# Denser side work in the first feed-forward, and split score products for four more head pairs

## The chip, the cores and the metric

The kernel runs on one core of one Trainium2 chip. The metric is the device time of one execution in microseconds; the time before is the median of three runs. The engines are TensorE (PE; its weight loads are listed as PEld), VectorE (DVE), ScalarE (ACT), GpSimd (POOL) and SyncE (SP), which issues the transfers.

## The reference, cut to what matters

```python
# attention over 8 batches, 12 heads, 448 tokens, head size 64, all float32
q_n, k_n = rmsnorm(q, g_q), rmsnorm(k, g_k)
scores = (q_n @ k_n.T) / sqrt(64)
attn = softmax(scores)
x = (attn @ v), heads side by side: (8, 448, 768)
# spectral mix, then a feed-forward layer
u = x + real(fft2(x))                  # over tokens and channels
un = (u - mean(u)) / sqrt(var(u) + 1e-6)
out = u + relu(un @ w_ch1) @ w_ch2     # 768 -> 3072 -> 768
```

## The kernel before, in words

**Batches and pairs.** Each of the eight batches goes through `aux` (attention, then the spectral mix) and then `ffn`. Attention works on six pairs of heads per batch. For a pair, `transpose_pair` loads q, k and v, normalizes q and k, turns them with TensorE and leaves `QT` and `KD`; `softmax_pair` makes the scores of four chunks of 112 tokens, with a minimum on DVE and an exponential on ACT for each head; `value_pair` turns the probabilities and multiplies them with v. `fold` and `spectral` do the Fourier part: products y, ab, transposes x, then the normalized rows `un`, whose sum of squares ACT takes in place over `u` after `u` has been stored to memory.

**Split and plain products.** A float32 value is cut into a rounded part and a remainder (type fp32r), and a product is made as a sum of fast products. In a split pair of scores (lines 322 to 348) ACT makes two rounded copies of q, two scaled ones of k and two copies of these into the other half, DVE makes two remainders of q and two of k; the remainder of k lies in one buffer that all pairs share, `KL`. The scores are two matmuls per head and chunk (line 375). In a plain pair (lines 302 to 320) ACT makes one copy of each, and the scores are one float32 matmul per head and chunk (line 372), which the trace shows as two instructions. Before the change, pairs 2 to 5 of the first batch are plain, by `PLAIN_SCORES`, which `plain_s` reads. The products with v are plain in batches 0 and 1 whatever that constant says (`PLAIN_PAIRS`).

**Feed-forward.** `ffn(b)` has 24 `up` products (line 908, 18 matmuls each) and 36 `down` products (line 929, 12 each), in six groups: one up first, then four ups and six downs per group, the last group with three ups. In `ffn(0)` the weights arrive as 64-bit floats and are converted piece by piece (`convert`, lines 701 to 730): a load into one of two buffers, two passes on ACT, three on DVE, one on POOL, one on ACT, one on DVE, and a store of the result (`kept`, line 758) for the later batches. 60 pieces are needed; 14 are converted during the first batch's attention.

**The order of the work.** `ffn(b)` is the main work, and `aux(b + 1)` is merged into it as side work. Both are generators that yield planned costs; an up counts 3420, a down 2280. The rule is in `merge`:

```python
done += cost
while side_done < done * ratio:
    x = next(side, None)
...
for _ in side:
    pass
```

What is left of the side work when the feed-forward is through runs behind it. The ratio is `RATIO_FIRST` for `ffn(0)` and `RATIO` (0.49) for the others. Before the merge, `AHEAD` = 14 steps of the second batch's side work are done along with the first batch's spectral mix. After `ffn(b)`, `ffn_input(b + 1)` turns the `un` rows for the next feed-forward. The framework orders the instructions of each engine by this program order and a planned timeline, when the kernel is built; on the chip each engine and SP's queue takes its instructions in that order.

Of the kernel before, what the change touches and what calls it, by code (L numbers as in the profile page):

```python
# [24 lines left out]
NPAIR = H // 2  # L25
# [12 lines left out]


RATIO = 0.49  # L40
RATIO_FIRST = 0.45
CONVERT_EARLY = 0.12
EARLY = 2
DFT_STEP = 40
AHEAD = 14
PLAIN_PAIRS = range(2 * NPAIR)
PLAIN_SCORES = range(2, NPAIR)
PACE = 3
LAG = 3

# [39 lines left out]
def spectral_block(ctx, tc, q, k, v, g_q, g_k, w1, w2, d1, d2, out, nb=B):  # L90
# [197 lines left out]
    def plain_s(b, p):  # L288
        return b * NPAIR + p in PLAIN_SCORES

# [396 lines left out]
    def aux(b):  # L687

        EO, uns[b] = [], {}
        yield from attention(b, EO)  # L690
        mixing.append(b)
        yield from spectral(b, xTs[b], EO, uns[b])
# [296 lines left out]
    for b in range(nb):  # L989
        merge(  # L990
            ffn(b, ffn_input(b, uns.pop(b))),
            second if b == 0 else aux(b + 1) if b + 1 < nb else iter(()),
            RATIO if b else RATIO_FIRST,
        )
# [21 lines left out]
```

## Time and profile before

| | |
|---|---|
| median of three runs | 2202.68 us (2202.3 to 2204.17) |
| the profiled execution's own time | 2202.25 us |
| its span, first to last instruction | 2200.5 us |
| mean granted TensorE clock | 0.977 |
| busy: PE, DVE, ACT, POOL | 96%, 70%, 48%, 16% |

The profile names groups of instructions by line, engine, operation and tile. A busy PE is not PE at its peak, since matmuls are pipelined and their ends are modelled: how fast TensorE really goes is read from the starts of its instructions. The stretch up to about 190 us is the first batch's attention and spectral mix; from there to 472.6 us is `ffn(0)`; from about 506 us each batch takes some 250 us.

### The profile page before, as it was taken

The page shows a single profiled execution, that of the slowest core. Times are in us where ns is not written, and L with a number is a line of the kernel's source. Part 1 is how long each engine was busy: PE and PEld are TensorE (multiplying, and loading weights), DVE is VectorE, ACT ScalarE, POOL GpSimd, SP SyncE. Part 2 cuts the span into 40 slices and gives each one's busy share as a digit, 9 for nine tenths or more (in the row PEclk, how much of TensorE's full clock was granted, in tenths as well). Part 3 has the DMA queues.
Part 4 walks back from the last instruction along what each step waited for, and adds up shares of the span by engine and source line. Part 5 has one row for each costly group of instructions (what it writes and reads, how often), then busy time and mean ns, then how long its engine had stood idle before and what let it go on. Part 6 is the DMA issues. An engine that isn't in the chain of part 4 may idle for free.

```text
span 2200.5 us, 31296 instructions
## 1 busy us (share of the span) xinstructions
PE 2118.1 (96%) x11224; PEld 1841.3 (84%) x11224; DVE 1541.8 (70%) x2987; ACT 1046.3 (48%) x2242; POOL 344.2 (16%) x196
## 2 busy tenths in 40 slices
PE   7977999989999999999999999999999999999997
PEld 4345777767999999999999999999999999998997
DVE  6678778766887588857787588857787588753122
ACT  7757766635553455525553355525553355422100
POOL 3323433311110011101110011101110011000000
PEclk8987999999999999999999999999999999999999
DMA  5546887846555675558556675568556674449665
GB/s 164 170 134 205 271 277 242 259 149 185 169 170 188 190 216 174 167 184 245 170 166 187 187 227 164 167 189 246 171 160 189 199 215 155 155 167 283 214 212 138
DMA packets 298301, 424.74 MB, mean 193 GB/s; under 512 B 186609, under 2 KB 224482, under 8 KB 298146
## 3 DMA queue, kind: packets, MB, share of 16 engines
q1 hardware_dynamic: 298146, 422.74, 62.9%
q8 instruction: 89, 1.46, 0.3%
q14 instruction: 66, 0.54, 0.1%
HBM read 362.89 MB, written 65.27 MB: 195 GB/s over the span
## 4 chain that ended last, share of the span: by engine, by line
PE 82%; DMA 5%; ACT 4%; DVE 4%; issue 1%; POOL 1%; SPq 1%; DVEq 0%; ACTq 0%; POOLq 0%
PE h L908 29%; PE o L929 29%; PE S L375 5%; PE av L483 4%; PE pt L471 4%; DMA dblw<-w 3%; PE av L449 2%; PE y L588 2%; PE qk L327 1%; ACT P L113 1%; PE pt L442 1%; DMA ur<-u_dram 1%; PE oT L874 1%; PE x L620 1%; DMA w<-w 1%
## 5 line engine op out<-in xcount | busy, mean ns | idle before, releaser
L929 PE MATMUL o<-hs,w 128*128 128x448 f32 x3456 | 790.3, 371 | 4.7 <-DMA w<-w 1.9
L908 PE MATMUL h<-unT,w 128*128 128x448 f32 x3456 | 776.8, 371 | 5.1 <-ACT unT L113 2.8
L908 PEld LDWEIGHTS h<-unT,w 128*128 128x128 f32 x3456 | 642.4, 189 | 58.9 <-ACT unT L113 3.7
L929 PEld LDWEIGHTS o<-hs,w 128*128 128x128 f32 x3456 | 638.4, 189 | 63.0 <-issue 3.8
L113 ACT ACTIVATE P<-S,mn 112x448 f32<-112x448 f32 x384 | 243.6, 637 | 199.5 <-DVE mn L113 182.4
L113 ACT ACTIVATE hs<-h 128x448 fp32r<-128x448 f32 x192 | 104.4, 544 | 323.5 <-PE h L908 322.1
L113 DVE TENSOR_REDUCE mn<-S 112x1 f32<-112x448 f32 x384 | 234.0, 619 | 30.9 <-PE S L375 27.0
L113 DVE SCALAR_TENSOR_TENSOR hs<-h,hs 128x448 fp32r<-128x448 f32 x192 | 119.4, 622 | 147.6 <-ACT hs L113 145.6
L113 DVE TENSOR_TENSOR acc<-o,acc 128x448 f32<-128x448 f32 x240 | 149.0, 621 | 103.1 <-PE o L929 100.5
L113 POOL TENSOR_TENSOR qkn<-raw 112x1024 f32<-112x1024 f32 x36 | 68.5, 1902 | 700.3 <-PE qk L327 431.8
L113 POOL TENSOR_TENSOR ss<-ss,nhalf 112x16 f32<-112x16 f32 x48 | 147.0, 3062 | 184.5 <-DVE ss L113 165.9
L113 ACT CAST T<-pt 128x448 fp32r<-128x448 f32 x216 | 112.9, 533 | 100.7 <-PE pt L471 99.2
L483 PE MATMUL av<-T,vhl 128*128 128x448 f32 x432 | 153.6, 384 | 0.1
L113 DVE TENSOR_TENSOR T<-pt,T 128x448 fp32r<-128x448 f32 x216 | 131.8, 619 | 27.4 <-ACT T L113 26.3
L375 PE MATMUL S<-KD,QT 128*112 128x448 f32 x352 | 138.7, 395 | 7.0 <-ACT bs L113 4.0
L375 PE MATMUL S<-rounded,QT 128*112 128x448 f32 x352 | 132.0, 376 | 0.0
L113 DVE TENSOR_SCALAR P<-P,sm 112x448 f32<-112x448 f32 x288 | 122.1, 462 | 4.2
L471 PE MATMUL pt<-ident,P 112*128 112x112 f32 x864 | 121.4, 259 | 0.0
L471 PEld LDWEIGHTS pt<-ident,P 112*128 112x128 f32 x864 | 102.4, 140 | 15.5
L726 POOL TENSOR_TENSOR magw<-magw,dblw 128x512 uint32<-128x512 uint32 (+1 forms) x46 | 78.9, 1716 | 156.0 <-DVE magw L722 97.9
L113 POOL TENSOR_TENSOR rstd<-st,nhalf 112x1 f32<-112x1 f32 (+2 forms) x32 | 19.5, 608 | 522.5 <-DVE st L113 508.1
L483 PEld LDWEIGHTS av<-T,vhl 128*128 128x128 f32 x432 | 80.8, 188 | 7.6 <-DVE T L113 0.5
(122 smaller groups left out, 2495.4 us busy)
## 6 DMA issues: line engine op xcount, KB each, us to landing
w<-w SPq DMA_DIRECT2D x192, 768.0 KB, 4.7
w<-w SPq DMA_DIRECT2D x288, 512.0 KB, 4.2
dblw<-w SPq DMA_DIRECT2D x28, 512.0 KB, 5.0
dblw<-w SPq DMA_DIRECT2D x18, 768.0 KB, 5.6
raw<-q SPq DMA_DIRECT2D x96, 112.0 KB, 3.6
raw<-k SPq DMA_DIRECT2D x96, 112.0 KB, 3.7
v<-v SPq DMA_DIRECT2D x96, 96.0 KB, 4.2
u_dram<-u SPq DMA_DIRECT2D x24, 336.0 KB, 2.9
```

The source lines that it names most:

```text
L113: ins = emit(*args, **kwargs)
L327: nc.tensor.transpose(pt[:, c * C : (c + 1) * C], qk[:, i, c].rearrange("t h d -> t (h d)"), ident[:C, :C],)
L375: ins = nc.tensor.matmul(s_, QT[:, h, cs], K[:, h], start=step == 0, stop=step == 1)
L442: nc.tensor.transpose(pt[:, c * C : (c + 1) * C], Pc[c][:, 512 * h + j * 128 : 512 * h + (j + 1) * 128], ident[:C, :C],)
L449: nc.tensor.matmul(av[:D, :S], vhl[:, j, h], T, start=j == 0, stop=False)
L471: nc.tensor.transpose(pt[:, c * C : (c + 1) * C], Pc[c][:, 512 * h + j * 128 : 512 * h + (j + 1) * 128], ident[:C, :C],)
L483: nc.tensor.matmul(av[:, :S], lv, T[:, i], start=(j == 0 and i == 0), stop=False)
L588: nc.tensor.matmul(o, src[:, par, t0 : t0 + n], D1[:, ri, par, cols], start=i != 1, stop=i != 0,)
L620: nc.tensor.transpose(xp[:n, i * 128 : (i + 1) * 128], src[:, 3 * half + i], ident)
L726: behind(nc.gpsimd.tensor_tensor(out=bits, in0=bits, in1=low, op=ALU.add))
L908: pace(nc.tensor.matmul(o, w[:, a, c], unT[c][:, z], start=n == 0, stop=n == 17))
L929: pace(nc.tensor.matmul(o, w[:, a, f], hs[4 * g + f][:, z], start=n == 0, stop=n == 11))
```

## The change

Two constants change. `RATIO_FIRST` goes from 0.45 to 0.6, and `PLAIN_SCORES` is empty, so that pairs 2 to 5 of the first batch take the split way of lines 322 to 348 and 374 to 379.

```diff
 RATIO = 0.49
-RATIO_FIRST = 0.45
+RATIO_FIRST = 0.6
 CONVERT_EARLY = 0.12
...
 PLAIN_PAIRS = range(2 * NPAIR)
-PLAIN_SCORES = range(2, NPAIR)
+PLAIN_SCORES = ()
 PACE = 3
```

## Rows read from the trace of the kernel before

**Rows 1.** The page, busy time of TensorE: share of the span, instructions.

```profile
PE 2118.1 (96%) x11224; PEld 1841.3 (84%) x11224; DVE 1541.8 (70%) x2987; ACT 1046.3 (48%) x2242; POOL 344.2 (16%) x196
```

**Rows 2.** Windows: stretch, length, busy PE, PEld, DVE, ACT, POOL, clock, DMA, GB/s.

```profile
189.50:472.60 283.10, 273.54 (x1284) 210.57 (x1284) 219.81 (x358) 182.16 (x349) 106.92 (x61) 0.98 0.79 258
...
189.50:390.00 200.50, 190.95 (x903) 147.81 (x904) 160.90 (x258) 139.86 (x268) 80.04 (x46) 0.97 0.80 266
...
472.60:505.90 33.30, 19.92 (x113) 16.28 (x114) 20.92 (x51) 15.33 (x32) 2.33 (x4) 0.87 0.27 79
...
750.00:1000.00 250.00, 249.88 (x1398) 229.27 (x1397) 189.76 (x382) 118.97 (x263) 31.95 (x17) 1.00 0.63 190
```

**Rows 3.** Timeline of TensorE, last down of the first feed-forward, early up of the second.

```profile
469.90 2.70 PE L929 MATMUL o<-hs,w 128*128 128x448 f32 x12
...
505.94 1.47 PE L908 MATMUL h<-unT,w 128*128 128x448 f32 x3
```

**Rows 4.** Timeline of TensorE in the second feed-forward: y first and last, un.

```profile
714.81 1.93 PE L588 MATMUL y<-D,eo 128*113 128x130 f32 x16
...
719.76 0.32 PE L588 MATMUL y<-D,tot 128*112 128x65 f32 x2
...
751.79 1.04 PE L820 MATMUL un<-ident,un 113*128 113x113 f32 x9
```

**Rows 5.** Chain of waits, 390 to 420 us: start, length, what.

```profile
401.31 0.77 PE pt L442 x8
402.08 3.67 PE h L908 x18
405.75 0.81 PE S L375 x4
...
410.21 1.65 PE av L449 x4
...
416.61 2.47 PE o L929 x12
```

**Rows 6.** SP's queue, 184 to 480 us: conversion loads, and its longest wait.

```profile
L709 SPq DMA_DIRECT2D dblw<-w x44: 367/384/921, 184.4 to 438.1; - x44
...
SPq L758 <- DVE w L728: 91.3, 34, 7.0
```

**Rows 7.** Groups of the whole kernel by shape, making of QT, KD and KL.

```profile
L113 DVE SCALAR_TENSOR_TENSOR rounded<-qk,gains,KD 64x448 fp32r<-64x448 f32 x88 | 60.0, 681 | 19.1 <-ACT KD L113 17.7
L113 ACT ACTIVATE KD<-qk,gains 64x448 fp32r<-64x448 f32 x88 | 55.5, 631 | 44.7 <-PE qk L327 32.6 <-DVE rounded L113 9.3
L113 DVE TENSOR_TENSOR QT<-qk,QT 64x448 fp32r<-64x448 f32 x88 | 54.8, 622 | 9.3 <-ACT QT L113 7.2
L113 ACT CAST KD<-KD 64x448 fp32r<-64x448 f32 x88 | 49.8, 565 | 2.4
L113 ACT CAST QT<-qk 64x448 fp32r<-64x448 f32 x88 | 46.4, 527 | 18.8 <-PE qk L327 18.3
L113 ACT ACTIVATE KD<-qk,gains 128x448 f32<-128x448 f32 x4 | 2.6, 642 | 0.0
L113 ACT COPY QT<-qk 128x448 f32<-128x448 f32 x4 | 2.2, 561 | 0.2 <-PE qk L307 0.2
```

**Rows 8.** First batch's attention: window of its plain pairs, timeline of plain scores.

```profile
43.20:146.90 103.70, 90.59 (x356) 37.87 (x354) 74.39 (x126) 77.85 (x172) 33.34 (x21) 0.92 0.50 150
...
89.77 1.76 PE L372 MATMUL S<-KD,QT 64*112 64x448 f32 x8
```

**Rows 9.** Timelines of DVE and POOL, 52 to 84 us; chain of waits at 488 us.

```profile
52.86 0.68 DVE L722 SCALAR_TENSOR_TENSOR magw2e<-dblw2e,magw2e 128x512 uint32<-128x512 uint32 x1
...
81.91 2.25 DVE L722 SCALAR_TENSOR_TENSOR magw2e<-dblw2e,magw2e 128x512 uint32<-128x512 uint32 x1
...
81.77 1.83 POOL L726 TENSOR_TENSOR magw1e<-magw1e,dblw1e 128x768 uint32<-128x768 uint32 x1 [5.83 <-DVE magw1e L722]
...
488.66 2.74 DMA u_dram<-u
```

## The prediction

> **What bounds the kernel now.** I read the busy times first: TensorE is busy for 96% of the span [rows 1], which says that it is the bound, but a busy PE can also be a slow one. So the windows come next. In the steady part PE is busy for 249.88 of 250 us at full clock [rows 2]: there every microsecond of TensorE work is one of time, and the change touches none of it. It touches two places in front of that, and each must be read by its own limit.
>
> The first is the stretch of ffn(0), 283.1 us, and the 33.3 us behind it [rows 2]. What TensorE needs there at full speed comes from the spacing of its instructions [rows 5]: 18 up matmuls take 3.67 us, 12 down matmuls 2.47, four instructions of a plain product with v 1.65 (0.90 per matmul where they stand in pairs; I take 0.45 an instruction), four score matmuls 0.81, eight transposes 0.77. By the code ffn(0) has 24 x 18 ups and 36 x 12 downs, 177 us. Six pairs of plain products with v are 96 instructions (two per matmul), 43 us; five pairs of scores, 80 matmuls, 16 us; some 240 transposes, 23 us. That is 259 of 283 us, so **24 us of TensorE time are lost inside ffn(0)**, though it shows as busy.
>
> Behind it, from the last down product to the first real up of the next feed-forward, 33.3 us pass [rows 2, 3]. What TensorE does there is the second batch's spectral mix: y, 5.3 us when nothing holds it up [rows 4], ab and x, 12 and 24 instructions, 4.7 us by rows 5; then un, 2.3 us, and 8 score matmuls of the third batch, 1.6 us. That is 14 us, so **19 us are lost in the gap**. At later boundaries un stands among the down products [rows 4], and nothing is lost.
>
> The code says why the gap is there. The second batch's side work counts 86,160 in planned cost (per pair 3040 for scores, 840 for transposes, 9020 for values; 8760 for the spectral mix). The 14 steps ahead take 3460, so 82,700 are left. ffn(0) counts 24 x 3420 + 36 x 2280 = 164,160; 0.45 of it is 73,872. So 8,828 are left over, which is the spectral mix, and it runs with nothing beside it.
>
> Why are 24 us lost inside? The conversion loads follow one another at (438.1 - 184.4) / 43 = 5.9 us, and SP's queue spends 91.3 us at the store of a converted piece, waiting for DVE's last step, with the next loads queued behind it [rows 6]. DVE is busy for 160.9 of the first 200.5 us [rows 2], a share of 0.80. So in much of ffn(0) the up and down products wait for weights whose conversion queues, on ACT and DVE, behind side work.
>
> **The change, part by part.**
>
> *Ratio 0.6.* It runs out at 82,700 / 0.6 = 137,833, that is after 84% of ffn(0); the spectral mix then lies beside feed-forward products, and the last down of group 5 and all of group 6 run without side work. Nothing is added: the work of the 316.4 us from 189.5 to 505.9 stays, and TensorE's part of it is 273 us. The floor is thus a gain of 43 us. What stands against it is DVE: it has 219.81 + 20.92 = 241 us of work there [rows 2], now in less time. I take the share that it reached in the very stretch in which conversions were on the chain, 0.80: 241 / 0.80 = 300 us, a **gain of 16.5 us**. In conversions, with the 25.8 us of group 6 (3 x 3.67 + 6 x 2.47) and 2.4 us for un behind the last load, 300 us mean that the loads go at 6.5 us each; every 0.1 us more or less is 4.3 us. The bounds: at 5.9 us as now the second feed-forward starts 40 us earlier; at 6.8 us nothing is gained.
>
> Moved with the spectral mix are its stores: four tiles of u, two transfers each, now in SP's queue between stores of converted weights. ACT's sum of squares, in place, waits for u's transfer, 2.74 us in the gap [rows 9], and behind it on ACT wait the evictions of the ups, for which TensorE has two banks, 3.67 us each. I cost this at nothing, since two ups cover it; the price without that cover is a rival below.
>
> *Split scores in four pairs of the first batch.* On ACT a split pair has 2 x 527 + 2 x 631 + 2 x 565 = 3446 ns, a plain one 561 + 642 = 1203 [rows 7]: four pairs add 9.0 us. On DVE 2 x 622 + 2 x 681 = 2.6 us a pair are new, 10.4 us in all. On TensorE two plain chunks take 1.76 us [rows 8], 0.88 each; split, 0.81 [rows 5]: 16 chunks save 1.1 us. The number of yields is the same, so the early conversions and the steps ahead stay where they are. No engine is full here: of 103.7 us ACT is busy for 77.85, DVE for 74.39 [rows 8]. ACT's addition meets an occupied ACT with its share, 0.75, so 6.8 us of 9.0 count; DVE's is covered but for the second remainder of k, 0.68 us, on which the pair's first scores wait: 2.7 us. With 1.1 saved, a **loss of 8.4 us**. The bounds are a gain of 1 us (all added work beside the products with v) and a loss of 18 us (all of ACT's and DVE's additions in series, less 1.1). I take the middle because the products with v of the pair before fill part of these waits.
>
> **The sum** is -16.5 + 8.4 = -8.1 us, on the profiled execution's own 2202.25 us: 2194 us. The median of the runs is 0.4 us above that execution, and I leave it aside.
>
> **The rivals.**
>
> *Conversions slow down (slower).* Every piece passes between ACT, DVE and POOL some seven times, and denser side work adds to the queue at each. The point that decides is the spacing of the loads: at 6.6 us the gain equals the loss of the split scores. With three more side instructions of 0.62 us met per piece, and two pieces under way, a piece costs 0.9 us more: 6.8 us and nothing gained, or 2211 us with the 8.4. For it: the queue behind DVE's last step is there already [rows 6]. Against it: between 390 and 438 us TensorE, not the conversion, was on the chain [rows 5], so the pipeline can go faster than 5.9.
>
> *DVE held up by POOL (no change).* The folds are 23 DVE instructions with both inputs in SBUF, and they move next to conversions, where POOL is busy for 106.92 of 283.1 us [rows 2]. One DVE instruction of 0.68 us took 2.25 us when a POOL addition of 1.83 us had begun 0.14 us before it [rows 9]. At a chance of 0.38 and up to 1.57 us each, 23 of them lose up to 14 us; with 10 us the sum is 2204 us. The Trainium skill, "SBUF — State Buffer", section "Who interferes with whom", says that a DVE instruction with two SBUF inputs and a GpSimd one that reads SBUF exclude each other, and that the later one blocks for the whole of the first. By that rule, the trace agrees: 0.14 + 2.25 ends 0.56 us after POOL's 1.83.
>
> *The u stores block ACT (slower).* If each of the four sits behind a weight store at its longest wait, 7.0 us [rows 6], plus 2.74 us, less 3.67 us for one bank's cover, 24 us are lost: 2218 us. Against it: most of the 34 waits there are far shorter, 91.3 / 34 = 2.7 us.
>
> *Conversions keep their pace (faster).* With loads at 5.9 us the gain is 40 us: 2171 us. It needs DVE at 241 / 276 = 0.87, more than any window above.
>
> **How the numbers follow.** The forecast gets 0.47, with its own range of 2184 to 2203 us (DVE's share from 0.78 to 0.82, the scores' loss from 5 to 13 us); slower conversions 0.22, the block by POOL 0.14, the stores 0.06, unchanged pace 0.11. A measurement of this kernel can tell about 0.2%, 4.4 us, from no change. Faster by more than that: nearly all of the forecast, the unchanged pace, a little of the POOL case, 0.58. Within it: the rest of the forecast and half of the POOL case, 0.13. Slower: 0.29. The range from 2176 to 2213 us leaves out most of the unchanged pace and the tail of the stores. That the merge does not do what its ratio says is unlikely: the leftover computed for 0.45 is just what the gap holds [rows 3].
>
> **What would show it.** Right: y of the second batch starts before the last down of ffn(0); from that down to the first dense up pass a few us; the conversion loads stand 6.4 to 6.6 us apart; DVE is at 0.80 from the start of ffn(0) to its end; ffn(0) starts some 8 us later than before. Wrong: loads at 6.8 us or more; ffn(0) starting at the same time as before, or 15 us later; ACT idle for long behind the u stores. If the steady batches no longer take 250 us, something else has changed.

## The result, and the profile after

| | before | after |
|---|---|---|
| median | 2202.49 us (2201.01 to 2204.17) | 2176.81 us (2175.25 to 2178.04) |
| ratio, 95% interval | | 0.9883 [0.9866, 0.9900] |
| span of the profiled execution | 2200.5 us | 2175.9 us |

The change gains 25.7 us. The forecast was 2194 us, a gain of 8: the direction was right, the size three times too small. The time lies 0.8 us inside the wide range (2176 to 2213 us) and outside the forecast's own (2184 to 2203). Where the 24.6 us between the two profiled spans lie can be read from four marks: the first up of `ffn(0)`, the first dense up of the second feed-forward, the third batch's y, and the end.

| stretch | before | after | difference | forecast |
|---|---|---|---|---|
| start to first up of `ffn(0)` | 189.5 | 185.9 | -3.6 | +8.4 |
| from there to the second feed-forward | 316.4 | 300.5 | -15.9 | -16.5 |
| from there to the third batch's y | 208.9 | 205.2 | -3.7 | 0 |
| from there to the end | 1485.7 | 1484.3 | -1.4 | 0 |

The second stretch, the ratio's, came out as summed; the first, the split scores', with the other sign. The marks of after are in these rows; first the ups (line 908: first and last start) and the conversion loads, each listed by its line.

```profile
L908 PE MATMUL h<-unT,w x162: 358/365/740, 185.9 to 274.5; 128*128 128x448 f32 x162
...
L709 SPq DMA_DIRECT2D dblw<-w x46: 367/384/1251, 154.7 to 454.7; - x46
```

The next rows are the timeline of TensorE in the kernel after, around the last down of `ffn(0)`, and its third batch's y.

```profile
438.07 3.58 PE L588 MATMUL y<-D,eo 128*113 128x130 f32 x16
...
465.63 0.36 PE L820 MATMUL un<-ident,un 113*128 113x113 f32 x2
...
483.94 2.60 PE L929 MATMUL o<-hs,w 128*128 128x448 f32 x12
486.37 0.37 PE L908 MATMUL h<-unT,w 128*128 128x448 f32 x1
...
691.63 1.93 PE L588 MATMUL y<-D,eo 128*113 128x130 f32 x16
```

y of the second batch, which stood behind the last down in the gap of 33.3 us of before [rows 2, 3], now starts 46 us ahead of it, and the next up follows the last down at once. (In the kernel before, a single up stands at 503.75 us, ahead of the dense ups at 505.9; from single up to single up the second stretch is 314.3 us before and 300.5 after.) The price of that is in the loads: 44 of the 46 belong to `ffn(0)`, the first at 180.7 us, so they stand (454.7 - 180.7) / 43 = 6.4 us apart, against 5.9 before [rows 6]. The forecast had said 6.5.

The windows of the kernel after have the columns of [rows 2]: the stretch from the start of `ffn(0)` to the second feed-forward, the steady part, and the attention stretch of [rows 8].

```profile
185.90:486.40 300.50, 287.25 (x1393) 221.46 (x1394) 245.88 (x409) 197.76 (x382) 106.56 (x65) 0.98 0.75 249
735.00:985.00 250.00, 249.43 (x1398) 229.03 (x1398) 189.13 (x383) 118.47 (x263) 31.48 (x16) 1.00 0.64 189
43.20:146.90 103.70, 83.60 (x361) 41.24 (x359) 85.68 (x147) 86.03 (x189) 35.08 (x21) 0.91 0.53 161
```

The steady part is as it was. In the first batch DVE's work grew from 74.39 to 85.68 us and ACT's from 77.85 to 86.03 [rows 8], as costed, and yet the stage ended earlier. That is what the experiments have to explain.

### The profile page after: what moved, and what is told of

Same layout as the page of the kernel before. It is cut to its first block, busy times and chain, and to the rows that moved or that the text cites. A ratio compares the mean times of both kernels' runs of the same rounds, so it can differ in the third digit from the quotient of the medians.

```text
span 2175.9 us, 31327 instructions
## 1 busy us (share of the span) xinstructions
PE 2099.5 (96%) x11224; PEld 1835.0 (84%) x11224; DVE 1557.7 (72%) x3003; ACT 1053.4 (48%) x2258; POOL 343.0 (16%) x196
## 4 chain that ended last, share of the span: by engine, by line
PE 82%; DMA 5%; ACT 5%; DVE 4%; issue 2%; POOL 1%; SPq 0%; DVEq 0%; POOLq 0%; ACTq 0%
PE o L929 30%; PE h L908 29%; PE S L375 6%; PE av L483 4%; PE pt L471 4%; DMA dblw<-w 3%; PE qk L327 1%; PE y L588 1%; DMA w<-w 1%; PE av L449 1%; PE oT L874 1%; ACT P L113 1%; PE x L620 1%; PE rem L430 1%; PE av L488 1%
## 5 line engine op out<-in xcount | busy, mean ns | idle before, releaser
L929 PEld LDWEIGHTS o<-hs,w 128*128 128x128 f32 x3456 | 636.8, 188 | 69.8 <-issue 10.2
L375 PE MATMUL S<-KD,QT 128*112 128x448 f32 x384 | 152.1, 398 | 13.0 <-ACT KD L113 9.4
L375 PE MATMUL S<-rounded,QT 128*112 128x448 f32 x384 | 142.5, 373 | 0.0
L726 POOL TENSOR_TENSOR magw<-magw,dblw 128x512 uint32<-128x512 uint32 (+1 forms) x46 | 76.2, 1656 | 165.3 <-DVE magw L722 88.5
L375 PEld LDWEIGHTS S<-KD,QT 128*112 128x112 f32 x384 | 69.2, 181 | 24.4 <-ACT KD L113 12.1
```

Source lines behind the costliest of these rows:

```text
L375: ins = nc.tensor.matmul(s_, QT[:, h, cs], K[:, h], start=step == 0, stop=step == 1)
L726: behind(nc.gpsimd.tensor_tensor(out=bits, in0=bits, in1=low, op=ALU.add))
L929: pace(nc.tensor.matmul(o, w[:, a, f], hs[4 * g + f][:, z], start=n == 0, stop=n == 11))
```

## The experiments

Twelve kernels ran, in three groups of four, and each group has its own runs of the kernel before beside it (medians 2203.97, 2205.16 and 2204.88 us, in the order below: parts and ratios; copies, forms and the DVE load; the rest). All edits below are made to the kernel after.

### How far single profiles can be trusted

Both kernels ran again, unchanged, in the last group.

> The kernel before once more, for the spread of the milestones between executions of one program: if the marks of ffn(0)'s start (189.5 us), of the first conversion load behind it and of the third batch's y (714.8 us) return within 1 us, differences of 3 us between kernels can be read from single profiles; if they differ by 3 us or more, the shift of 3.6 us of the start from before to after is within the spread.

> The kernel after once more, on the same chip as the other three, for the same purpose: ffn(0) starts at 185.9 us and the third batch's y at 691.6 us, within 1 us, if single profiles can be compared; the time 2175 to 2178 us, some 26 us under before.

Before took 2210.18 us in its single run here; after took 2180.04 (2178.84 to 2180.67), ratio 0.9891 [0.9875, 0.9908]. The ups of the two, by line:

```profile
L908 PE MATMUL h<-unT,w x179: 360/364/742, 190.7 to 299.9; 128*128 128x448 f32 x179
```

```profile
L908 PE MATMUL h<-unT,w x162: 358/366/739, 185.1 to 275.9; 128*128 128x448 f32 x162
```

`ffn(0)` starts at 189.5 and 190.7 us before, at 185.9 and 185.1 after: 1 us of spread, so the shift of some 4 to 6 us is more than the spread. Later marks spread more: the third batch's y came at 714.8 and 716.4 us before, at 691.6 and 694.6 after, 3 us where 1 was expected. Differences of less than that in this mark say nothing.

### One part at a time

```diff
-PLAIN_SCORES = ()
+PLAIN_SCORES = range(2, NPAIR)
```

> The ratio of 0.6 alone; pairs 2 to 5 of the first batch stay plain. Theory A (the two parts add, each as the traces of before and after show it: ffn(0) begins 3.6 us earlier with split scores, and everything from there to the third batch's y is 19.6 us shorter with the ratio): about 20 us faster than before, 2180 to 2185 us, ffn(0) beginning at 189.5 us. Rival B (the split scores do cost 8 us, as the prediction had it, and the ratio gives 33): about 2169 us.

```diff
-RATIO_FIRST = 0.6
+RATIO_FIRST = 0.45
```

> Split scores alone; the ratio stays at 0.45. Theory A: ffn(0) begins at about 186 us, the gap behind ffn(0) stays at some 33 us, time 2197 to 2200 us. Rival B: 2207 to 2211 us.

| kernel | median, us | ratio | first up | to second feed-forward |
|---|---|---|---|---|
| ratio alone | 2188.15 | 0.9915 [0.9895, 0.9935] | 190.4 | 301.5 |
| split scores alone | 2186.69 | 0.9915 [0.9892, 0.9938] | 183.2 | 305.7 |

Each part alone gains 16 to 17 us; Theory A (some 20 and 5) and Rival B both missed. The last column goes to the first single up, for which the kernel before has 314.3. The split scores bring `ffn(0)` 6 to 7 us forward, so their loss of 8.4 us is refuted. The two gains add up to 33 us, and both together bring 25 to 26: they overlap, and the timelines show where. In the kernel with split scores alone, the last downs, TensorE's y (line 588) and the second feed-forward's first dense up stand so, with the idle time before them in brackets:

```profile
459.77 4.03 PE L929 MATMUL o<-hs,w 128*128 128x448 f32 x19
466.01 2.15 PE L588 MATMUL y<-D,eo 128*113 128x130 f32 x16 [2.21 <-DVE eo L113]
...
490.80 0.85 PE L908 MATMUL h<-unT,w 128*128 128x448 f32 x3
```

Its gap is 490.8 - 463.8 = 27.0 us, where before had 33.3 between the same marks. The window of it, with the columns of [rows 2]:

```profile
463.80:490.80 27.00, 18.29 (x113) 14.45 (x114) 18.95 (x48) 14.33 (x29) 1.78 (x3) 0.94 0.32 101
```

DVE has 48 instructions left in the gap instead of 51, and the clock is 0.94 instead of 0.87: more of the folds had already run ahead of the last down (four at most are left behind it in DVE's timeline, against seven in the kernel before). The order in which the framework sets each engine's instructions follows from a planned timeline; that a different first batch gave a different order 250 us later is the likely reason, not a tested one. So 33.3 - 27.0 = 6.3 us of the gap that the ratio closes were closed already, most of the overlap of the two parts, 7 to 8 us.

### How much ratio is needed

Only `RATIO_FIRST` differs: 0.51, then 0.75.

> Split scores, ratio 0.51: the side work runs out after 98.8% of ffn(0), so nothing is left behind it, and per step of ffn(0) it is 15% less dense than at 0.6. Theory A1 (what the ratio gives is the filled gap, the density within ffn(0) matters little): within 4 us of the changed kernel, 2173 to 2181 us. Rival C (conversions queue behind side work, so that density has a price of its own): loads of weights closer together than at 0.6 and 5 to 10 us faster, 2167 to 2172 us. Rival D (the end of the side work is a chain of waits that needs room behind it): slower by 5 us or more, 2182 us and up.

> Split scores, ratio 0.75: the side work runs out after 67% of ffn(0). Theory A1: within 4 us of the changed kernel. Rival C: the loads of weights further apart while the side work lasts, 7 us and more, and at the end ffn(0) alone, bound by conversions: 2185 to 2195 us.

0.51: 2184.20 us, ratio 0.9891 [0.9867, 0.9916]; the last down products end about 475 us and the dense ups begin at 492, so part of the spectral mix is still exposed, although the count of its plan left nothing behind. Rival D expected such a chain at the end, but the runs spread from 2178 to 2190 us, and the intervals of 0.51 and 0.6 overlap: the time does not tell the two apart. 0.75: 2179.13 us, 0.9879 [0.9858, 0.9899], loads 6.5 us apart, the same time as 0.6. Above 0.6 nothing more is gained, and nothing is lost either: the side work packed denser still did not bring the slower time that two of the rivals priced.

### What the copies cost

ACT's two copies of k into the other half are made three times in the four pairs: 16 more copies of 0.565 us, 9.0 us, as much as the change itself adds on ACT.

```diff
-                A.copy(KD[hi, 0], KD[lo, 0].bitcast(F32))
-                A.copy(KD[lo, 1], KD[hi, 1].bitcast(F32))
+                for _ in range(3 if b == 0 and p > 1 else 1):
+                    A.copy(KD[hi, 0], KD[lo, 0].bitcast(F32))
+                    A.copy(KD[lo, 1], KD[hi, 1].bitcast(F32))
```

> The changed kernel with ACT's two copies of k into the other half made three times instead of once in pairs 2 to 5 of the first batch: 4 x 4 x 0.565 = 9.0 us more on ACT, as much as the change itself added there, all in front of the pair's first scores. Prediction's pricing (an addition to ACT counts with ACT's share, three quarters and more): about 7 us slower than the changed kernel, ffn(0) beginning at 190 us or later. Theory P (the stage has room for it, the additions run beside the products with v): 0 to 2 us, ffn(0) beginning at 183 to 187 us as in the runs with split scores.

2191.92 us, 0.9934 [0.9918, 0.9950]; `ffn(0)` starts at 197.4 us, 11.5 us later than in after. TensorE's timeline in it has two waits of a length that after doesn't have (its longest from 43 to 118 us is 2.77):

```profile
52.12 1.75 PE L450 MATMUL av<-T,v 128*64 128x448 f32 x2 [5.07 <-ACT T L113]
75.14 1.75 PE L450 MATMUL av<-T,v 128*64 128x448 f32 x2 [5.46 <-ACT T L113]
```

So on top of the kernel after, more work on ACT is paid for in full, and more. Part of that may be TensorE's clock: it was granted 0.84 from 43.2 to 118 us here, against 0.95 and 0.93 in the two profiles of after. And it is the price where ACT is already full; what the same work costs in the kernel before is another question, which the next run bears on.

### The form of the product, the copies apart

Here the split copies are made, but the scores of the four pairs are one float32 matmul per head over 64 rows; the products with the remainders are left out.

```diff
                 for step, K in enumerate((KD, KL)):
...
+                if b == 0 and p > 1:
+                    nc.tensor.matmul(
+                        s_, QT[hs, h, cs].bitcast(F32), KD[hs, h].bitcast(F32),
+                        start=True, stop=True,
+                    )
+                    continue
```

(The added lines stand ahead of the loop.)

> The changed kernel with all copies and remainders of the split way made as now, but in pairs 2 to 5 of the first batch the scores are one float32 matmul per head and chunk over 64 rows, of the rounded q and the rounded k: the products with the remainders are left out. Theory M (what the split scores won in the first batch is won on TensorE: the float32 score matmuls on half the rows take longer and go with a longer stretch at half clock): the gain is gone, ffn(0) begins at 189 us or later, 4 to 8 us slower than the changed kernel. Theory O (it is won by the order in which the instructions come, or by ACT and DVE): ffn(0) begins at 183 to 187 us, within 2 us of the changed kernel.

2190.20 us, 0.9930 [0.9909, 0.9950]; `ffn(0)` starts at 192.6 us, 6.7 us later than in after, and 2 to 3 us later than in before. The split way's copies and remainders, with plain products, therefore cost 2 to 3 us, where the prediction had 9.5; and among these copies the plain form starts `ffn(0)` 7 us later than the split one, where the prediction had 1.1. Now the windows of 10 us, with the columns of [rows 2]; the last but two is the granted clock. First this kernel:

```profile
50.00:60.00 10.00, 9.78 (x20) 3.65 (x21) 7.09 (x12) 5.52 (x15) 5.23 (x3) 0.56 0.46 159
60.00:70.00 10.00, 10.00 (x18) 2.77 (x16) 2.82 (x7) 5.36 (x13) 0.00 (x0) 0.50 0.40 107
70.00:80.00 10.00, 10.00 (x34) 4.81 (x33) 5.61 (x10) 7.22 (x12) 2.07 (x2) 0.74 0.22 63
```

The same stretch of the kernel before:

```profile
50.00:60.00 10.00, 9.07 (x22) 3.67 (x22) 7.96 (x15) 6.09 (x18) 4.23 (x2) 0.66 0.55 184
60.00:70.00 10.00, 9.85 (x40) 4.27 (x38) 3.09 (x7) 6.75 (x13) 0.86 (x2) 0.83 0.35 96
70.00:80.00 10.00, 8.90 (x42) 3.89 (x38) 8.37 (x16) 8.17 (x21) 4.78 (x2) 1.00 0.51 145
```

And of the kernel after:

```profile
50.00:60.00 10.00, 8.31 (x29) 3.80 (x28) 8.98 (x15) 8.34 (x21) 4.08 (x2) 0.83 0.56 179
60.00:70.00 10.00, 9.25 (x50) 5.21 (x48) 7.55 (x16) 9.78 (x21) 3.10 (x3) 1.00 0.65 176
70.00:80.00 10.00, 7.29 (x23) 3.80 (x24) 7.52 (x13) 8.39 (x21) 3.50 (x2) 0.83 0.58 174
```

With plain matmuls TensorE is "busy" for all of 60 to 70 us with 18 instructions, at a clock of 0.50, which is the 1.2 GHz level; ACT is busy for half of it. After the change TensorE gets 50 instructions through in the same ten microseconds at 1.00, and ACT is full. A busy share alone doesn't tell these two apart. What TensorE does in the slow stretch is in this kernel's timeline:

```profile
50.22 1.00 PE L375 MATMUL S<-KD,QT 64*112 64x448 f32 x2 [1.76 <-ACT KD L113]
...
52.05 1.83 PE L375 MATMUL S<-KD,QT 64*112 64x448 f32 x2
...
60.63 1.83 PE L375 MATMUL S<-KD,QT 64*112 64x448 f32 x2
```

One head of a chunk, when it stands alone, is 1.00 us at full clock and 1.83 at half. The prediction's price of a plain chunk, 0.88 us for both heads [rows 8], was read from a place where two chunks stand together and the heads share TensorE.

### More plain pairs

```diff
-PLAIN_SCORES = ()
+PLAIN_SCORES = range(NPAIR)
```

> The changed kernel with all six pairs of the first batch plain, where the kernel before had four. Theory M: the later start of ffn(0), 4 us for four pairs, grows with the pairs: 190 to 193 us. Prediction's pricing: two pairs more of ACT's and DVE's work saved, so ffn(0) begins some 4 us earlier than in the kernel before, at 185 us.

2185.76 us, 0.9905 [0.9886, 0.9925]. The theory that plain matmuls are slow in themselves (M) expected a late start, 190 to 193 us. The prediction's pricing, by which two pairs less of ACT's and DVE's work save 4 us against before, expected 185. It came at 184.8 us, as early as with all six pairs split:

```profile
L908 PE MATMUL h<-unT,w x162: 359/365/739, 184.8 to 273.9; 128*128 128x448 f32 x162
```

So Theory M missed and the pricing hit, and neither form as such starts `ffn(0)` earlier. The windows show another reason that would do as well. The same three as above, for this kernel:

```profile
50.00:60.00 10.00, 9.36 (x46) 4.11 (x43) 8.98 (x18) 9.03 (x25) 5.21 (x3) 1.00 0.61 174
60.00:70.00 10.00, 9.57 (x43) 4.09 (x44) 4.50 (x9) 7.48 (x13) 1.29 (x1) 1.00 0.39 116
70.00:80.00 10.00, 8.96 (x37) 3.30 (x35) 10.00 (x18) 9.97 (x27) 5.58 (x2) 1.00 0.51 152
```

Six plain pairs in another order, and the clock stays up. The clock and the saved ACT work differ together here, and the run cannot tell them apart. (The time is still some 7 us above after's: the stretch behind the start took 308.9 us, against 300.5.)

### More work for TensorE

```diff
-                for step, K in enumerate((KD, KL)):
+                both = (KD, KL) * (2 if b == 0 and p > 1 else 1)
+                for step, K in enumerate(both):
...
```

> The kernel after, with the split score products of the first batch's pairs 1 to 5 issued twice into the same accumulation, so those scores come out doubled: 20 chunks x 0.81 us = 16 us more for TensorE (13 us of it in the four pairs that the change touches), nothing more for the other engines. Theory M (TensorE's time in the first batch counts nearly one for one, so the plain matmuls' slower form was the mis-sized term): ffn(0) starts 8 to 16 us later than the 185.9 us of after, at 194 to 202, and the time is 8 to 16 us above after, 2185 to 2193. Theory O (the stage goes by the other engines and TensorE's added work lies beside them; plain matmuls lost by their order and their waits, not by their length): ffn(0) starts at most 4 us later, and the time is within 4 us of after. The prediction's own sum, with every microsecond of TensorE counted there, sides with M.

(The edit doubles four pairs, 2 to 5, so it adds 16 chunks x 0.81 = 13 us; the expectation's 20 chunks and 16 us count a pair too many. In the trace TensorE is busy with score products for 30.14 us from 43.2 to 118 us, against 18.90 in after: 11.2 more.) It took 2173.37 us (2171.72 to 2176.37), ratio 0.9863 [0.9848, 0.9878]: with 11 us more to do, 7 us under the kernel after in the same group. `ffn(0)` starts at 184.7 us, not at 194 or later; that is as Theory O had it, though the time is not within its 4 us:

```profile
50.00:60.00 10.00, 9.02 (x41) 4.98 (x40) 8.22 (x13) 8.41 (x22) 4.03 (x2) 1.00 0.52 165
60.00:70.00 10.00, 9.35 (x45) 4.91 (x45) 7.18 (x13) 8.63 (x17) 1.99 (x2) 1.00 0.54 164
70.00:80.00 10.00, 8.57 (x43) 5.62 (x42) 8.60 (x16) 8.57 (x22) 5.13 (x2) 1.00 0.48 130
...
184.70:481.10 296.40, 286.56 (x1405) 223.09 (x1405) 247.06 (x412) 197.43 (x384) 104.80 (x65) 0.98 0.76 252
```

Theory M falls: the amount of TensorE's work in the split first batch did not move the start. That is not because another engine sets the pace: TensorE has 47.2 us of this kernel's chain of waits from 43.2 to 118 us, ACT 13.0. But TensorE ran at a clock of 1.00 throughout. What this kernel gains on after lies behind the start: the stretch to the second feed-forward took 296.4 us instead of 300.5 and 304.3 in the two profiles of after, with the same work in it. Over all kernels with the ratio at 0.6 and the same work there, this stretch runs from 296.4 to 308.9 us (doubled scores, after, ratio alone 301.5, more copies 302.4, plain products 303.7, after again, six plain pairs). TensorE's timelines show another order at its end; that the order makes the difference is likely and was not tried by itself.

### DVE's work in `ffn(0)`

First more of it: three pairs of the second batch take the split way for the products with v, 24 us more on DVE and 13 us less on TensorE; the ratio is set to 0.53 for the larger planned cost.

```diff
-RATIO_FIRST = 0.6
+RATIO_FIRST = 0.53
...
-PLAIN_PAIRS = range(2 * NPAIR)
+PLAIN_PAIRS = range(9)
```

> The changed kernel with the products with v of pairs 3 to 5 of the second batch split as in the later batches, and the ratio at 0.53, so that the smaller planned cost of the side work again runs out at about 83% of ffn(0). Per pair TensorE's work falls by 4.4 us, and DVE gets 0.7 + 4 x 0.62 + 6 x 0.62 + 2 x 0.62 = 8.1 us more, 24 us in all. Theory D (DVE, at a share of 0.80, sets the length of ffn(0)): 25 to 30 us slower than the changed kernel. Rival T (TensorE's work sets it): some 13 us faster. Rival C (the spacing of the conversions sets it, and DVE only through what queues in front of them): in between, 0 to 15 us slower.

Then less: one of the three DVE passes of a conversion is left out.

```diff
-        behind(nc.vector.scalar_tensor_tensor(
-            out=bits, in0=high, scalar=0xC0000000, in1=bits,
-            op0=ALU.bitwise_and, op1=ALU.bitwise_or,
-        ))
+        if starting[0]:
+            behind(nc.vector.scalar_tensor_tensor(
+                out=bits, in0=high, scalar=0xC0000000, in1=bits,
+                op0=ALU.bitwise_and, op1=ALU.bitwise_or,
+            ))
```

> The kernel after without one of the three DVE passes of a conversion (the merge of the sign and the top exponent bits) for the pieces converted during ffn(0): the converted weights lack those bits. DVE has some 28 x 0.77 + 17 x 0.96 = 38 us less between the start of ffn(0) and the second feed-forward, TensorE the same. If DVE's work, or a piece's passage through it, sets the length of that stretch (the step of the prediction that took 241 us / 0.80 = 300 us): the stretch falls from 300.5 us towards TensorE's floor of 273, by 10 to 27 us, the loads stand 5.8 to 6.2 us apart, and the time is 2150 to 2167 us. If only the gap that was filled mattered and the 27 us above the floor are lost in another way (order of the products, waits for banks): within 4 us of after.

More DVE work: 2186.57 us, 0.9910 [0.9887, 0.9933], against 2176.81 and 2180.04 of after. Less: 2173.58 us (2171.84 to 2176.80), 0.9864 [0.9849, 0.9879], which is 6.5 us under after in the same group. The intervals of the first and of after's two measurements overlap. The windows from the first up to the second feed-forward, first with more, then with less:

```profile
183.10:490.00 306.90, 277.94 (x1387) 230.64 (x1387) 255.42 (x434) 199.29 (x381) 105.11 (x64) 0.96 0.74 246
```

```profile
185.00:477.90 292.90, 284.33 (x1392) 219.70 (x1393) 211.98 (x355) 193.13 (x375) 97.38 (x64) 0.99 0.78 256
```

By the trace the first kernel has 255.42 - 245.88 = 9.5 us more of DVE work in the stretch, not the 24 expected, and the stretch is 6.4 us longer than after's 300.5 (2.6 longer than its second profile's). That lies in the range of Rival C, between DVE's share alone and TensorE's work alone; but 306.9 also lies within the 296.4 to 308.9 us that the same work takes in other kernels, so it shows no price. In the second, 34 us less of DVE work (211.98 against 245.88) shortened the stretch by 7.6 us against after's 300.5, or 11.4 against its second profile; the median gained 6.5. The loads stand (445.5 - 178.7) / 43 = 6.2 us apart, at the edge of the 5.8 to 6.2 that DVE's bound called for; the stretch and the time (2150 to 2167 us) fell short of it, and the time is not within the other theory's 4 us either. The gain is also no more than the doubled scores gained without any change in DVE. If DVE's share were a law, 211.98 / 0.80 = 265 us would lie under TensorE's floor of 273, and the stretch would be at that floor. DVE's share came out at 0.83 with more work, 0.82 in after and 0.72 with less, so the share follows the work; it is no fixed limit that sets the time.

## Why the prediction was right, and where it was wrong

**Right in its range, by luck.** The sum had -16.5 us for the ratio and +8.4 for the split scores. The first is what the ratio alone gave; the second had the wrong sign, and the time stayed in the range with 0.8 us to spare only because the two gains overlap. The total lies nearer to the 2171 us of the rival with unchanged pace than to 2194; only the spacing of the loads tells them apart.

**Right: where the time was lost, and what the ratio is worth.** The gap of 33.3 us closed, un stands among the down products, the loads went to 6.4 us (said: 6.5), DVE's share to 245.88 / 300.50 = 0.82 (said: 0.80), and the stretch to 300.5 us (said: 300). As the ratio alone, 16 us of gain, against 16.5 in the sum. That the stretch hit within 1 us is chance: the same kernel's second profile has 304.3.

**Right in its number, not shown as a cause: DVE as the bound.** The step 241 us / 0.80 took a share reached in one stretch as what DVE can reach. With 34 us less, the stretch moved by 7.6 / 34 to 11.4 / 34, some 0.2 to 0.3 us for each microsecond of DVE work, not by 1 / 0.80; and at 292.9 us it is just 3.5 below a kernel whose DVE work was untouched. What else holds a piece up was not separated: it passes ACT and POOL too, and SP's queue in the kernel after (184 to 500 us) waits 80.0 us with loads for POOL's step, 72.3 us with stores for DVE's last.

**Wrong: "a loss of 8.4 us" for the split scores.** The start of `ffn(0)` moved forward: the three profiles with plain pairs 2 to 5 and no added copies have it at 189.5, 190.7 and 190.4 us, eight with split scores and no added copies at 183.1 to 185.9, so 3.6 to 7.6 us earlier. The term for TensorE, "16 chunks save 1.1 us", was nearly right. Both its prices are the cheapest rows, but the forms compare alike where they stand. The windows of the score products alone, 43.2 to 118 us (busy PE, PEld, clock, DMA, GB/s), are for before, after and six plain pairs, one line each:

```profile
43.20:118.00 74.80, 21.06 (x64) 7.06 (x64) 0.93 0.54 161
```

```profile
43.20:118.00 74.80, 18.90 (x65) 10.56 (x64) 0.95 0.53 161
```

```profile
43.20:118.00 74.80, 18.65 (x64) 5.93 (x64) 0.98 0.53 162
```

The 16 chunks take 21.1 us plain and 18.9 split, 2.2 less; with the clock up, plain ones take 18.7, and with the copies beside them 29.5 (43.2 to 130 us, at a clock of 0.84). With 2.2 for 1.1 the sum for the start is still +7.3. The step that failed is the other one: ACT's and DVE's additions were laid on the path, 6.8 + 2.7 = 9.5 us, by ACT's average share and with the words that no engine is full here. With plain products the same additions cost 2 to 3 us; with split ones the start came earlier. The working had [rows 8] with a clock of 0.92 before it and no term for the missing 0.08, nor for a stretch in which TensorE alone is late. The chain of waits of the kernel before has that stretch (start, length, what):

```profile
51.93 1.00 PE S L372 x2
52.94 1.40 PE pt L442 x8
54.33 3.26 PE S L372 x4
57.59 1.68 PE av L449 x2
59.27 0.94 PE pt L442 x4
60.21 1.69 PE av L449 x2
61.90 0.94 PE pt L442 x4
```

From 51.93 to 65.4 us the end is set by TensorE alone, at half clock for most of it: four instructions of plain scores take 3.26 us there, where eight take 1.76 in [rows 8], and products with v 1.68 instead of 0.90. In the kernel after, the chain runs over ACT from 84.83 to 88.5 us, and again from 90.1 to 98 us; the first rows of it:

```profile
84.83 0.51 ACT w2e L727
85.34 0.43 ACT T L113
85.77 0.52 ACT KD L113
86.29 0.95 ACT qkn L113
87.27 0.56 ACT KD L113
```

The same for all of 43.2 to 118 us, with the pieces of the chain summed:

| kernel | TensorE's part of the chain, us | clock | first up |
|---|---|---|---|
| before, twice; ratio alone | 30.8, 29.5; 32.6 | 0.93, 0.92; 0.92 | 189.5, 190.7; 190.4 |
| after, twice; split alone | 17.0, 18.5; 20.6 | 0.95, 0.93; 0.95 | 185.9, 185.1; 183.2 |
| plain products with the copies | 53.0 | 0.82 | 192.6 |
| more copies | 36.7 | 0.84 | 197.4 |
| six plain pairs | 30.9 | 0.98 | 184.8 |
| doubled scores | 47.2 | 1.00 | 184.7 |

So the change takes TensorE off part of the chain, 9 to 16 us of it. ACT's part is 28.6 and 21.4 us before and 31.5 and 29.9 after, where ACT is busy for 70.50 of the 74.8 us. The clock alone is not the cause: before and the second profile of after have the same 0.93 and start 4.4 us apart. TensorE on the chain alone is not either, by the last two rows. The start is late in just those kernels in which TensorE has 29 us or more of the chain and a clock of 0.93 or less as well. That is a reading of ten profiles, not a test: between before and six plain pairs the windows above lose (0.34 + 0.17) x 2 x 10 = 10.2 us of half clock, worth at most half of that, 5.1 us, and the start moved by 4.7, but so it should by the saved ACT work. No run held the clock and changed nothing else, and why the start gained where the sum had a loss stays open in part.

Late in the kernel after is a conversion at the end of the attention: ACT waits 5.27 us for POOL at 137 us, and TensorE 6.21 behind it. Behind these the chain goes back to a transfer of v in the one profile (6.61 us from 124.50) and to one of a weight in the other (4.32 us from 127.47). The timeline has the two waits in these rows:

```profile
137.24 0.62 ACT L727 CAST w2e<-magw2e 128x512 fp32r<-128x512 f32 x1 [5.27 <-POOL magw2e L726]
...
138.35 1.76 PE L449 MATMUL av<-T,v 128*64 128x448 f32 x2 [6.21 <-ACT T L113]
```

**Wrong: that the parts simply add.** They overlap by 7 to 8 us, because the split scores alone had already shortened the gap to 27.0 us. The prediction had no term for the order of the instructions; the stretch of `ffn(0)` with the same work differs by up to 12 us between kernels, 4 of them between two profiles of one kernel. The after-effect of the change on the second feed-forward, 3.7 us, had no term either; it stands in both profiles of after, and its cause wasn't tried.

**The rivals.** Conversions slowed from 5.9 us to 6.4 and 6.5 (0.6 and 0.75), not to the 6.6 and 6.8 of the rival; nor did the stores of u hold ACT up, which waits 1.6 us for them in all. DVE held up by POOL is there but small: between the same two marks DVE has 409 instructions in both kernels, 219.81 + 20.92 = 240.73 us before [rows 2] and 245.88 after, 5.2 us longer, against the 10 us of that rival. The Trainium skill, "SBUF — State Buffer", section "Who interferes with whom", would have DVE instructions with two SBUF inputs wait where they meet POOL's. By that rule, the trace agrees in direction: of the 5.2 us, the folds have 2.4. The unchanged pace of 5.9 us did not come about: 6.4.

## What to carry to other kernels

Price both forms of an operation in the stage at hand, not by their cheapest rows: a chunk of scores was priced at 0.88 and 0.81 us, and took 1.3 and 1.2 in place. An addition to an engine is not paid by its average share: ask what the chain of waits runs over there, and read the granted clock beside the busy share. Ten microseconds with 18 instructions and ten with 50 both showed a TensorE that was 93 to 100% busy. A stage whose chain runs over TensorE at half clock may gain from a form that gives other engines more work, as this one did. Where a framework orders instructions by a plan, an edit can also reshuffle later stages; here the same work took 296.4 to 308.9 us, a spread as large as the effects under study, so a difference of that size needs a second edit that reaches it by another way.

## What the runs showed of the hardware that was not expected

With 11.2 us of added score products in the first batch the granted clock was 1.00 from 43.2 to 118 us (0.95 and 0.93 in the two profiles of after, 0.93 and 0.92 before), and `ffn(0)` started no later; there is one profile of it. Ahead of the fall near 53 us in the kernel before, TensorE was busy for 1.35 and 1.17 us of two stretches of 2 us, with 7 and 4 instructions; with the doubled scores for 1.76 and 1.39 us of the same, with 11 and 9, and the clock stayed. But with the doubled scores the stretch ahead of these, 47 to 49 us, has only 0.87 us with 6 instructions, and the clock stayed all the same, so these rows do not show what the fall hangs on.

The price of a 64-row float32 product depends on its neighbours: eight instructions of two heads take 1.76 us together [rows 8], two of one head alone 1.00 us, and 1.83 at half clock. The Trainium skill, "TensorEngine Tiling (Array Packing)", section "Key Properties", says that different tiles of the array can load weights and multiply in parallel. By that, the trace agrees, the two heads being 64 rows each: 0.22 us an instruction with the other head beside it, 0.50 without.
